# Second batch's dense layers in two chunks of 384 rows instead of three of 256

## The chip, the cores and the metric

The kernel runs on one core of one Trainium2 chip. The metric is the device time in microseconds; the time before is the median of three runs.

## The reference, cut to what matters

Three layers follow each other for a batch of 2, 768 rows each: an attention in which a row sees a window of earlier rows and the first few (sinks), a dense pair with a convolution over three neighbouring rows as a gate, and four attention experts of which each row uses two. The middle layer is the one that the change touches:

```
h = np.maximum(x @ w_in, 0.0)                    # x: 2 x 768 x 512, h: 2 x 768 x 1024
hp = pad h by one row of zeros on either side
for k in range(3):
    conv_out += conv_w[k][None, None, :] * hp[:, k:k + S, :]
gate = 1.0 / (1.0 + np.exp(-conv_out))
y = (h * gate @ w_out).astype(np.float32)        # 2 x 768 x 512
```

Then the third layer takes y: for each expert q, k, v by y @ wq[e], y @ wk[e], y @ wv[e], a causal softmax, @ v @ wo[e], weighted by a softmax over the two largest of four gate logits of the row.

## The kernel before

Features lie on the 128 partitions and rows run along the free axis. Every product of two matrices is made from three matmuls: both operands are split into a high part and a low part (`xh`, `xl`; `winhf`, `winlf`), and high x high, high x low and low x high are summed in one accumulator bank. The helper `hilo` makes such a pair: ScalarE copies the source into the high part, VectorE subtracts that from the source into the low part; `hilo_later` puts the subtraction on a list that is run one step later.

A batch's 768 rows are cut into chunks of CH = 256 rows. One **dense step** is one chunk c and one block f of 128 of the 1024 hidden features. Its parts are:

- H (`m1_H`, line 753): 4 input blocks x 3 = 12 matmuls of XW = 258 columns (256 rows and one neighbour on either side) into one bank. Then ScalarE does the relu (line 756) and, in the second batch, the product with the middle tap (line 758); in the first batch GpSimd has that product (line 760).
- conv (`m1_conv`): two VectorE instructions add the left and the right tap (lines 766, 767), then ScalarE's tanh (line 769).
- gate (`m1_gate`): VectorE forms (1 + tanh) x h (line 774), ScalarE copies it into the high part of g (line 776).
- rest (`m1_rest`, line 782): GpSimd makes the low part of g.
- Y (`m1_Y`, line 797): 4 output blocks of 128 x 3 = 12 matmuls of 256 columns into two banks, two output blocks in each, summed over the eight steps of the chunk. After the last one the sum is split into `yh` and `yl` (`hilo_later`, lines 130 and 131).

The order is written by hand: `run_phases` walks through steps and calls, at each step, the parts of all phases in the order of a list (ORD1), each part for its own step minus its lag. For the dense phase LAGM = (1, 2, 3) puts conv one step, gate two and rest three after the H of the same block, and LAG_Y puts its Y four after. So a step of this phase has one H, one conv, one gate and one Y of four different blocks. The first batch has 24 dense steps (its chunks in two halves of four blocks, so that weights can arrive late); the halves' sums are added on VectorE (line 815), cast on ScalarE (line 823), and the low part is taken on GpSimd (line 819). The second batch has 3 chunks x 8 blocks = 24 steps.

Beside the dense work `misc` runs at each step. From w0 = 32 on (i counts dense steps) it loads and splits the projections' weights, and at i = w0 it calls `narrow`: VectorE compares a guard tile and sums it (lines 188, 189), TensorE adds that over the partitions by one small matmul with a column of ones (line 191), and VectorE forms a flag from it (line 192). The flag decides at the end whether a second, general program has to run; it does not run here.

Buffers come from rings: W (18), R (15, for `xh`, `xl`, `yh`, `yl`), K (2 large ones, first the keys and later the projection weights), and eight accumulator banks (`psB`).

Of the kernel before, what the change touches and what calls it, by code (L numbers as in the profile page):

```python
# [29 lines left out]
E = 4  # L30
# [34 lines left out]
LAG_Y = 4  # L65
# [23 lines left out]
class Kernel:  # L89
# [508 lines left out]
    def xt(self, b, c):  # L598

        if (b, c) not in self.x:  # L600
            self.x[(b, c)] = (self.Rt([P, NKC, XW], s="xh"), self.Rt([P, NKC, XW], s="xl"))
            for edge, col in ((0, 0), (NCH - 1, XW - 1)):
                if c == edge:
                    for x in self.x[(b, c)]:
                        self.nc.gpsimd.memset(x[:, :, col : col + 1].bitcast(F32), 0.0)
        return self.x[(b, c)]

    def x_cols(self, qt):
        return slice(1 + (qt % 2) * P, 1 + (qt % 2 + 1) * P)

    def x_hi(self, b, qt, general=False):
        self.copy("a" if general else ENG_XH[b], self.xt(b, qt // 2)[0][:, :, self.x_cols(qt)], self.a1O[(b, qt)])

    def x_lo(self, b, qt, general=False):
        xh, xl = (x[:, :, self.x_cols(qt)] for x in self.xt(b, qt // 2))
        eng = self.nc.vector if general or ENG_X[b] == "d" else self.nc.gpsimd
        eng.tensor_tensor(xl, self.a1O.pop((b, qt)), xh.bitcast(F32), op=ALU.subtract)

    def x_halo(self, b, qt):
        c = qt // 2  # L620
        if qt % 2 == 0 and c > 0:
            for d, x in zip(self.xt(b, c - 1), self.xt(b, c)):
                self.nc.gpsimd.tensor_copy(d[:, :, XW - 1 : XW], x[:, :, 1:2])
        if qt % 2 == 1 and c < NCH - 1:
            for d, x in zip(self.xt(b, c + 1), self.xt(b, c)):
                self.nc.gpsimd.tensor_copy(d[:, :, 0:1], x[:, :, XW - 2 : XW - 1])

# [117 lines left out]
    def m1_H(self, b, c, f):  # L745
        nc = self.nc
        xh, xl = self.x[(b, c)]
# [6 lines left out]
        ht = self.Wt([P, XW + CH], s="ht")  # L754
        h, t1 = ht[:, :XW], ht[:, XW:]
        nc.scalar.activation(h, ps[:, :XW], AF.Relu, scale=0.5)  # L756
        if TAP == "a" or (TAP == "b" and b == 1):
            nc.scalar.mul(t1, h[:, 1 : 1 + CH], self.cw[:, NF + f : NF + f + 1])
        else:
            nc.gpsimd.tensor_scalar(t1, h[:, 1 : 1 + CH], self.cw[:, NF + f : NF + f + 1], 1.0, op0=ALU.mult, op1=ALU.mult)  # L760
        self.m1h[(b, c, f)] = (h, t1)

    def m1_conv(self, b, c, f):
        nc = self.nc
        h, t1 = self.m1h[(b, c, f)]
        nc.vector.scalar_tensor_tensor(t1, h[:, 0:CH], self.cw[:, f : f + 1], t1, op0=ALU.mult, op1=ALU.add)
        nc.vector.scalar_tensor_tensor(t1, h[:, 2 : 2 + CH], self.cw[:, 2 * NF + f : 2 * NF + f + 1], t1,  # L767
# [3 lines left out]
    def m1_gate(self, b, c, f):  # L771
        nc = self.nc
        h, t1 = self.m1h.pop((b, c, f))
        nc.vector.scalar_tensor_tensor(t1, t1, 1.0, h[:, 1 : 1 + CH], op0=ALU.add, op1=ALU.mult)  # L774
        g = self.Wt([P, 2, CH], F32R, "g")
        nc.scalar.copy(g[:, 0], t1)  # L776
        self.m1g[(b, c, f)] = (t1, g)

    def m1_rest(self, b, c, f):
        t1, g = self.m1g[(b, c, f)]  # L780
        eng = self.nc.vector if ENG_G[b] == "d" else self.nc.gpsimd
        eng.tensor_tensor(g[:, 1], t1, g[:, 0].bitcast(F32), op=ALU.subtract)  # L782
        self.m1g[(b, c, f)] = g

    def m1_Y(self, b, c, f):
# [6 lines left out]
        first, last = f == 0 or (halves and f == NF // 2), f == NF - 1 or (halves and f == NF // 2 - 1)  # L792
        if first:
            self.m1y = [self.psB().rearrange("p (a c) -> p a c", a=2) for _ in range(2)]
        for d in range(NKC):
            for i, (w, k) in enumerate(((wh, 0), (wh, 1), (wl, 0))):
                nc.tensor.matmul(self.m1y[d // 2][:, d % 2, :], w[:, f, d, :], g[:, k],  # L797
                                 start=(first and i == 0 and d % 2 == 0), stop=(last and i == 2),
                                 skip_group_check=True)
        if not last:  # L800
            return
# [26 lines left out]
    def mlp_phase(self, start):  # L828
# [29 lines left out]
        def each(fn):  # L858
# [430 lines left out]
```

## Time and profile before

| | before |
|---|---|
| median of 3 runs | 371.82 us (371.38 to 372.03) |
| profiled run | 371.99 us |
| its span | 370.1 us |
| TensorE busy | 359.7 us, 3166 matmuls |
| VectorE busy | 273.1 us |
| ScalarE busy | 261.2 us |
| GpSimd busy | 118.8 us |

The span is the time from the first to the last instruction on record; 1.9 us of the profiled run lie outside it. Matmuls overlap each other, so the time that one of them takes from the path is the distance from its start to the next one's start, not the duration in its row.

### The profile page before, as it was taken

How to read it: one execution, taken by the hardware profiler on the slowest of the kernel's cores; microseconds unless marked ns; L12 is line 12 of the kernel's file. 1: busy time of each engine (PE TensorE's matmuls, PEld its weight loads, DVE VectorE, ACT ScalarE, POOL GpSimd, SP SyncE). 2: the span in 40 equal slices, each digit the busy share in tenths (PEclk: the TensorE clock that was granted, in tenths of full speed). 3: DMA queues.
4: the chain of work that ended last, by engine and by line, in shares of the span. 5: the costliest groups of instructions: out<-in, count | busy, mean ns of one | idle time of the engine just before them, and what ended most of it. 6: DMA issues, size and time to landing. Idle time of an engine off the chain costs nothing.

```text
span 370.1 us, 8877 instructions
## 1 busy us (share of the span) xinstructions
PE 359.7 (97%) x3166; PEld 331.7 (90%) x3166; DVE 273.1 (74%) x850; ACT 261.2 (71%) x746; POOL 118.8 (32%) x230
## 2 busy tenths in 40 slices
PE   8999999899999999999999999999999999999994
PEld 5687877899899999999999999999999899978983
DVE  5689899999887997878756766238668688578731
ACT  4999998766886766546746766249878687849841
POOL 7014120444432342844421322500034144406310
PEclk9999999999999999999999999999999999999998
DMA  7943865353342311000211010000000010101112
GB/s 178 362 140 126 241 220 173 116 186 129 103 128 69 105 30 31 6 25 25 63 44 45 1 58 3 0 2 0 2 3 1 17 42 22 40 0 58 58 51 75
DMA packets 20404, 27.53 MB, mean 74 GB/s; under 512 B 2080, under 2 KB 12928, under 8 KB 20352
## 3 DMA queue, kind: packets, MB, share of 16 engines
q1 hardware_dynamic: 19120, 26.22, 22.2%
q10 hardware_dynamic: 1232, 0.66, 0.9%
q8 instruction: 27, 0.44, 0.5%
q14 instruction: 25, 0.20, 0.2%
HBM read 23.68 MB, written 3.19 MB: 73 GB/s over the span
## 4 chain that ended last, share of the span: by engine, by line
PE 77%; DVE 12%; ACT 5%; issue 2%; POOL 2%; DMA 1%; SPq 0%; ACTq 0%; DVEq 0%
PE psB L797 15%; PE psB L753 14%; PE psB L947 9%; PE psB L1061 5%; PE psB L1037 5%; PE psB L875 5%; PE psB L1085 4%; PE psB L587 4%; PE psB L484 4%; PE psB L545 3%; DVE P L486 3%; PE psB L1008 3%; PE psB L1007 3%; PE psB L471 2%; ACT P L489 2%
## 5 line engine op out<-in xcount | busy, mean ns | idle before, releaser
L797 PE MATMUL psB<-g,wouthf 128*128 128x256 f32 x384 | 70.5, 281 | 0.2 <-POOL g L782 0.2
L797 PEld LDWEIGHTS psB<-g,wouthf 128*128 128x128 f32 x384 | 58.9, 188 | 0.6 <-POOL g L782 0.4
L753 PE MATMUL psB<-xh,winhf 128*128 128x258 f32 x192 | 56.5, 294 | 0.0
L1025 POOL TENSOR_SCALAR P<-P,r 128x256 f32<-128x256 f32 (+5 forms) x48 | 30.3, 644 | 79.4 <-DVE r L1023 32.6
L753 PE MATMUL psB<-xh,winlf 128*128 128x258 f32 x192 | 54.3, 283 | 0.0
L753 PE MATMUL psB<-xl,winhf 128*128 128x258 f32 x192 | 54.2, 282 | 0.0
L797 PE MATMUL psB<-g,woutlf 128*128 128x256 f32 x192 | 53.8, 280 | 0.0
L489 ACT ACTIVATE P<-P,nm 128x260 f32<-128x260 f32 (+2 forms) x96 | 46.5, 486 | 10.1 <-DVE nm L486 9.9
L782 POOL TENSOR_TENSOR g<-ht,g 128x256 fp32r<-128x256 f32 x48 | 33.2, 691 | 52.4 <-ACT g L776 46.9
L1014 ACT ACTIVATE P<-P,nm 128x256 f32<-128x256 f32 (+5 forms) x48 | 32.1, 669 | 13.5 <-DVE nm L1013 7.8
L769 ACT ACTIVATE ht<-ht 128x256 f32<-128x256 f32 x48 | 20.1, 418 | 28.3 <-DVE ht L767 28.2
L774 DVE SCALAR_TENSOR_TENSOR ht<-ht 128x256 f32<-128x256 f32 x48 | 24.2, 505 | 18.8 <-ACT ht L769 18.8
L753 PEld LDWEIGHTS psB<-xh,winhf 128*128 128x128 f32 x192 | 36.4, 189 | 0.3 <-ACT ht L756 0.2
L753 PEld LDWEIGHTS psB<-xl,winhf 128*128 128x128 f32 x192 | 36.5, 190 | 0.0
L753 PEld LDWEIGHTS psB<-xh,winlf 128*128 128x128 f32 x192 | 36.2, 189 | 0.0
L797 PEld LDWEIGHTS psB<-g,woutlf 128*128 128x128 f32 x192 | 36.2, 189 | 0.0
L1010 DVE CUSTOM_DVE_ANT_0 P<-psB,causal 128x384 f32<-128x384 f32 (+3 forms) x64 | 30.3, 503 | 5.7 <-PE psB L1008 5.2
L760 POOL TENSOR_SCALAR ht<-ht,cw 128x256 f32<-128x256 f32 x24 | 15.1, 627 | 59.8 <-ACT ht L756 52.3
L767 DVE SCALAR_TENSOR_TENSOR ht<-ht,cw 128x256 f32<-128x256 f32 x48 | 28.3, 589 | 1.7
L545 PE MATMUL psB<-ident,P 128*128 128x128 f32 x176 | 29.0, 281 | 0.2
L947 PE MATMUL psB<-yh,wqh 128*128 128x256 f32 x96 | 27.2, 283 | 0.0
L947 PE MATMUL psB<-yl,wqh 128*128 128x256 f32 x96 | 27.0, 281 | 0.0
(172 smaller groups left out, 961.3 us busy)
## 6 DMA issues: line engine op xcount, KB each, us to landing
raw<-in_w_in_dram SPq DMA_DIRECT2D x8, 512.0 KB, 4.1
raw<-in_w_out_dram SPq DMA_DIRECT2D x8, 512.0 KB, 3.3
v<-in_v_dram SPq DMA_DIRECT2D x12, 256.0 KB, 4.4
R<-rD SPq DMA_DIRECT2D x24, 128.0 KB, 2.9
out_dram<-ot SPq DMA_DIRECT2D x11, 256.0 KB, 2.0
k<-in_k_dram SPq DMA_DIRECT2D x7, 260.0 KB, 3.6
raw<-in_wqkv_dram SPq DMA_DIRECT2D x8, 193.0 KB, 3.0
q<-in_q_dram SPq DMA_DIRECT2D x6, 256.0 KB, 4.5
```

The costliest lines, as they stand in the source:

```text
L489: nc.scalar.activation(Pt[:, j, :N], Pt[:, j, :N], AF.Exp, bias=nmx[:, j : j + 1], scale=-1.0, accum_out=sums[:, j : j + 1])
L545: nc.tensor.transpose(ps[:, j, c, :], Pt[:, j, c0 : c0 + P], self.ident)
L753: nc.tensor.matmul(ps[:, :XW], w[:, f, kc, :], x[:, kc, :], start=(i == 0), stop=(i == len(ops) - 1))
L767: nc.vector.scalar_tensor_tensor(t1, h[:, 2 : 2 + CH], self.cw[:, 2 * NF + f : 2 * NF + f + 1], t1, op0=ALU.mult, op1=ALU.add)
L769: nc.scalar.activation(t1, t1, AF.Tanh)
L774: nc.vector.scalar_tensor_tensor(t1, t1, 1.0, h[:, 1 : 1 + CH], op0=ALU.add, op1=ALU.mult)
L782: eng.tensor_tensor(g[:, 1], t1, g[:, 0].bitcast(F32), op=ALU.subtract)
L797: nc.tensor.matmul(self.m1y[d // 2][:, d % 2, :], w[:, f, d, :], g[:, k], start=(first and i == 0 and d % 2 == 0), stop=(last and i == 2), ...
L947: nc.tensor.matmul(ps, w[:, kc, c0 : c0 + P], y[:, kc, :], start=(i == 0), stop=(i == len(ops) - 1))
L1010: nc.vector.tensor_tensor_reduce(out=Pt[:, lo:hi], in0=ps[:, : hi - lo], in1=mask, scale=-1.0, scalar=BIG, op0=ALU.add, op1=ALU.min, accum ...
L1014: nc.scalar.activation(Pt[:, :N], Pt[:, :N], AF.Exp, bias=nm[:, 0:1], scale=-1.0, accum_out=sums[:, j : j + 1])
L1025: nc.gpsimd.tensor_scalar(Ps[j][:, :N], Ps[j][:, :N], r[:, j : j + 1], 1.0, op0=ALU.mult, op1=ALU.mult)
```

## The change

In the second batch a chunk has 384 rows (`TPC` = 3 tiles of 128 instead of 2), so there are 2 x 8 = 16 dense steps instead of 24. H has 386 columns, Y has 384 and one bank for each output block, four banks instead of two. Each bank is drained in two pieces, 256 and 128 columns, since `yh` and `yl` stay cut by 256 rows, and the subtraction is made at once instead of a step later. The second batch's lags are (0, 1, 2, 3): the convolution of a block comes in the step of its own H. `w0` is four steps earlier, 28 instead of 32, and with it `narrow`. The phase is cut into m (first batch), n (second batch) and z (`misc` and background work).

The rest is about room: the second chunk's x lies in one large K buffer that held keys, its first chunk's x in tiles of two input blocks each, `h`, `t` and the two parts of g in buffers of their own, the low projection weights in three R tiles, the first batch's queries in the K buffer after x, all values in one pool, the zeros in W. The neighbour columns of x are copied when the tile on the right is there, both directions at once.

```diff
-LAGM = (1, 2, 3)
+LAGM = ((1, 2, 3, 4), (0, 1, 2, 3))
     def x_halo(self, b, qt):
...
+        c, n = qt // TPC[b], TPC[b] * P
+        if qt % TPC[b] or c == 0:
+            return
+        for ls, rs in zip(self.xt(b, c - 1), self.xt(b, c)):
+            for (g, l), (_, r) in zip(ls, rs if len(rs) == len(ls) else [(0, rs[0][1][:, g : g + l.shape[1]]) for g, l in ls]):
+                self.nc.gpsimd.tensor_copy(l[:, :, n + 1 : n + 2], r[:, :, 1:2])
+                self.nc.gpsimd.tensor_copy(r[:, :, 0:1], l[:, :, n : n + 1])
     def m1_H(self, b, c, f):
...
+        n = TPC[b] * P
-            nc.tensor.matmul(ps[:, :XW], w[:, f, kc, :], x[:, kc, :], start=(i == 0), stop=(i == len(ops) - 1))
+            nc.tensor.matmul(ps[:, : n + 2], w[:, f, kc, :], x[kc], start=(i == 0), stop=(i == len(ops) - 1))
     def m1_Y(self, b, c, f):
...
+        per = 1 if b else 2
         if first:
-            self.m1y = [self.psB().rearrange("p (a c) -> p a c", a=2) for _ in range(2)]
+            self.m1y = [self.psB()[:, : per * TPC[b] * P].rearrange("p (a c) -> p a c", a=per) for _ in range(NKC // per)]
...
+        if b:
+            tiles = range(c * TPC[b], (c + 1) * TPC[b])
...
+            for d in range(NKC):
+                for k in sorted({t // 2 for t in tiles}):
+                    mine = [t for t in tiles if t // 2 == k]
+                    dst = slice(mine[0] % 2 * P, (mine[-1] % 2 + 1) * P)
+                    src = self.m1y[d][:, 0, (mine[0] - tiles[0]) * P : (mine[-1] + 1 - tiles[0]) * P]
+                    yh, yl = self.y[(b, k)]
+                    self.hilo(src, yh[:, d, dst], yl[:, d, dst])
+            return
     def mlp_phase(self, start):
...
-        steps += [(1, c, f) for c in range(NCH) for f in range(NF)]
-        w0 = NSTEP + NF
+        steps1 = [(1, c, f) for c in range(NT // TPC[1]) for f in range(NF)]
+        w0 = NSTEP + NF // 2
...
-            if w0 + 3 <= i < w0 + 3 + 2 * NKC:
-                self.hilo_later(*self.wraw.pop(i - w0 - 3))
+            if w0 + 2 <= i < w0 + 2 + 2 * NKC:
+                for part in self.wraw.pop(i - w0 - 2):
+                    self.hilo_later(*part)
...
+        n0 = start + len(steps)
+        total = len(steps) + len(steps1)
+        z = {"more": (0, more), "misc": (0, misc)}
+        return (phase(start, steps, LAGM[0]), phase(n0, steps1, LAGM[1]),
+                lambda names: (start, total, [z[n] for n in names.split()], 1), start + total)
```

What stands in a row on VectorE around the guard, before. L766 and L767 are the two convolution instructions, L774 the gate, L188 and L189 the guard, L192 the flag; the block whose tile is `ht_2845` had its H one step earlier than the H that TensorE has just done:

```order
L774 SCALAR_TENSOR_TENSOR ht_2810<-ht_2810 128x256 [waits Activation_49]
L766 SCALAR_TENSOR_TENSOR ht_2845<-ht_2845,cw 128x256 [waits Pool_49]
L767 SCALAR_TENSOR_TENSOR ht_2845<-ht_2845,cw 128x256 [waits DVE_49]
L188 TENSOR_SCALAR guard<-guard 128x17
L189 TENSOR_REDUCE g_2901<-guard 128x1 [waits DVE_49]
L192 SCALAR_TENSOR_TENSOR flag<-psB_2904,c_831 1x1 [waits PE_49]
```

And in the changed kernel, where L785 and L786 are the convolution, L794 the gate, L189, L190 and L193 the guard and the flag; `t_2774` belongs to the H that TensorE has just done, and L852 adds the halves of the first batch's last chunk:

```order
L852 TENSOR_TENSOR y_2078<-psB_2593,y_2078 128x512 [waits PE_49]
L852 TENSOR_TENSOR y_2078<-psB_2594,y_2078 128x512 [waits PE_49]
L785 SCALAR_TENSOR_TENSOR t_2715<-h_2714,cw,t_2715 128x384 [waits Activation_49]
L786 SCALAR_TENSOR_TENSOR t_2715<-h_2714,cw,t_2715 128x384 [waits DVE_49]
L794 SCALAR_TENSOR_TENSOR t_2715<-t_2715,h_2714 128x384 [waits Activation_49]
L785 SCALAR_TENSOR_TENSOR t_2774<-h_2773,cw,t_2774 128x384 [waits Activation_49]
L786 SCALAR_TENSOR_TENSOR t_2774<-h_2773,cw,t_2774 128x384 [waits DVE_49]
L189 TENSOR_SCALAR guard<-guard 128x17
L190 TENSOR_REDUCE g_2798<-guard 128x1 [waits DVE_49]
L193 SCALAR_TENSOR_TENSOR flag<-psB_2801,c_831 1x1 [waits PE_49]
```

The guard stands behind two convolutions in both; what moved is whose convolutions they are, those of the H of the step before, or of this step's own.

On TensorE at the same place, before, the end of a Y (L797), the small matmul (L191) and the next H (L753):

```order
L797 MATMUL psB_2743<-g_2814,wouthf 128x256 x2
L797 MATMUL psB_2743<-g_2814,woutlf 128x256
L797 MATMUL psB_2743<-g_2814,wouthf 128x256 x2
L797 MATMUL psB_2743<-g_2814,woutlf 128x256
L191 MATMUL psB_2904<-ones,g_2901 1x1 [waits DVE_49,PE_49]
L753 MATMUL psB_2912<-xh_1592,winhf 128x258
```

And in the changed kernel, a Y (L822), the small matmul (L192) and the next H (L768):

```order
L822 MATMUL psB_2740<-g_2681,woutlf 128x384
L822 MATMUL psB_2741<-g_2681,wouthf 128x384
L822 MATMUL psB_2741<-g_2682,wouthf 128x384
L822 MATMUL psB_2741<-g_2681,woutlf 128x384
L192 MATMUL psB_2801<-ones,g_2798 1x1 [waits DVE_49,Activation_49]
L768 MATMUL psB_2811<-xh_1244,winhf 128x386 [waits PE_49]
```

The small matmul keeps its place between a Y and the next H; the Y ahead of it has 384 columns in each matmul instead of 256.

## Rows read from the trace of the kernel before

**Rows 1.** Page, parts 1 and 2: busy us (share) xinstructions; granted clock in tenths.

```profile
PE 359.7 (97%) x3166; PEld 331.7 (90%) x3166; DVE 273.1 (74%) x850; ACT 261.2 (71%) x746; POOL 118.8 (32%) x230
...
PEclk9999999999999999999999999999999999999998
```

**Rows 2.** Page, part 4: chain that ended last, by engine.

```profile
PE 77%; DVE 12%; ACT 5%; issue 2%; POOL 2%; DMA 1%; SPq 0%; ACTq 0%; DVEq 0%
```

**Rows 3.** Windows: stretch, length, then busy us (instructions) by engine, clock, DMA.

```profile
183.00:230.00 47.00, 47.00 (x397) 46.84 (x396) 30.84 (x66) 30.42 (x78) 11.04 (x16) 1.00 0.12 34
```

**Rows 4.** Timeline, TensorE, an H group: start us, duration us, instruction.

```profile
227.56 0.28 PE L753 MATMUL psB<-xh,winhf 128*128 128x258 f32 x1
...
229.00 0.40 PE L797 MATMUL psB<-g,wouthf 128*128 128x256 f32 x2
```

**Rows 5.** Timeline, TensorE, third layer: 256, 384 and 512 columns.

```profile
293.60 0.28 PE L947 MATMUL psB<-yh,wqh 128*128 128x256 f32 x1
...
295.02 0.82 PE L1037 MATMUL psB<-ident,P 128*128 128x128 f32 x6
...
295.86 0.34 PE L1008 MATMUL psB<-KS,QL 128*128 128x384 f32 x1
...
297.10 0.28 PE L947 MATMUL psB<-yh,wqh 128*128 128x256 f32 x1
...
299.87 0.63 PE L1085 MATMUL psB<-wohf,zh 128*128 128x512 f32 x2
...
301.27 0.34 PE L1007 MATMUL psB<-KS,QH 128*128 128x384 f32 x1
...
301.97 0.28 PE L947 MATMUL psB<-yh,wqh 128*128 128x256 f32 x1
```

**Rows 6.** Timeline, VectorE, around the guard.

```profile
185.97 0.48 DVE L767 SCALAR_TENSOR_TENSOR ht<-ht,cw 128x256 f32<-128x256 f32 x1
...
186.57 0.17 DVE L189 TENSOR_REDUCE g<-guard 128x1 f32<-128x17 f32 x1
```

**Rows 7.** Timeline, TensorE, around the small matmul.

```profile
183.05 0.40 PE L797 MATMUL psB<-g,wouthf 128*128 128x256 f32 x2
...
187.21 0.28 PE L797 MATMUL psB<-g,woutlf 128*128 128x256 f32 x1
187.41 0.19 PE L191 MATMUL psB<-ones,g 128*1 128x1 f32 x2
```

**Rows 8.** Timeline, ScalarE, at a convolution, an H and a chunk end.

```profile
164.97 0.42 ACT L769 ACTIVATE ht<-ht 128x256 f32<-128x256 f32 x1 [2.44 <-DVE ht L767]
...
183.31 0.39 ACT L756 ACTIVATE ht<-psB 128x258 f32<-128x258 f32 x1 [0.45 <-PE psB L753]
...
218.96 1.07 ACT L130 CAST yh<-psB 128x512 fp32r<-128x512 f32 x2
221.81 0.42 ACT L769 ACTIVATE ht<-ht 128x256 f32<-128x256 f32 x1 [1.78 <-DVE ht L767]
```

**Rows 9.** Groups, ScalarE, 183 to 230 us: xcount | busy us, mean ns.

```profile
L758 ACT ACTIVATE ht<-ht,cw 128x256 f32<-128x256 f32 x17 | 8.7, 512 | 0.6
...
L130 ACT CAST wqh<-raw 128x386 fp32r<-128x386 f32 x8 | 4.0, 499 | 0.0
```

**Rows 10.** Groups, VectorE, the same stretch.

```profile
L131 DVE TENSOR_TENSOR wql<-raw,wqh 128x386 fp32r<-128x386 f32 x8 | 4.5, 558 | 0.0
L131 DVE TENSOR_TENSOR yl<-psB,yh 128x512 fp32r<-128x512 f32 x4 | 2.6, 686 | 4.4 <-ACT yh L130 4.4
```

**Rows 11.** Timeline, VectorE, beside the low parts on GpSimd.

```profile
162.24 1.25 DVE L766 SCALAR_TENSOR_TENSOR ht<-ht,cw 128x256 f32<-128x256 f32 x1
163.53 1.41 DVE L767 SCALAR_TENSOR_TENSOR ht<-ht,cw 128x256 f32<-128x256 f32 x1
```

**Rows 12.** Timeline, GpSimd, the low parts of one chunk.

```profile
161.90 2.75 POOL L819 TENSOR_TENSOR yl<-y,yh 128x512 fp32r<-128x512 f32 x2 [0.48 <-ACT yh L823]
```

**Rows 13.** Timeline, GpSimd, a copy of neighbour columns.

```profile
137.22 0.38 POOL L626 CAST xl<-xl 128x4 fp32r<-128x4 f32 x1 [0.76 <-DVE xl L617]
```

More of the change, by code (lines that the diff above doesn't have):

```diff
@@ L64 @@
 RATE1 = 1.1
-LAG_Y = 4
 NP2BUF = 8
@@ L600, in xt @@
         if (b, c) not in self.x:
-            self.x[(b, c)] = (self.Rt([P, NKC, XW], s="xh"), self.Rt([P, NKC, XW], s="xl"))
-            for edge, col in ((0, 0), (NCH - 1, XW - 1)):
+            w = TPC[b] * P + 2
+            if b and c:
+                t = self.Kt([P, 2, NKC, w], F32R, "x")
+                self.x[(b, c)] = [[(0, t[:, i])] for i in range(2)]
+            else:
+                n = NKC if b == 0 else NKC // 2
+                self.x[(b, c)] = [[(g, self.Rt([P, n, w], s="x" + s)) for g in range(0, NKC, n)] for s in "hl"]
@@ L619, in x_halo @@
+        self.a1O.pop((b, qt))
     def x_halo(self, b, qt):
[L620 to L626, printed above, removed]
+        c, n = qt // TPC[b], TPC[b] * P
+        if qt % TPC[b] or c == 0:
+            return
@@ L746, in m1_H @@
         nc = self.nc
-        xh, xl = self.x[(b, c)]
+        xh, xl = ([x[:, i] for _, x in part for i in range(x.shape[1])] for part in self.x[(b, c)])
         wh, wl = self.win
@@ L773, in m1_gate @@
         h, t1 = self.m1h.pop((b, c, f))
-        nc.vector.scalar_tensor_tensor(t1, t1, 1.0, h[:, 1 : 1 + CH], op0=ALU.add, op1=ALU.mult)
-        g = self.Wt([P, 2, CH], F32R, "g")
-        nc.scalar.copy(g[:, 0], t1)
+        n = TPC[b] * P
+        nc.vector.scalar_tensor_tensor(t1, t1, 1.0, h[:, 1 : 1 + n], op0=ALU.add, op1=ALU.mult)
+        if b:
+            g = [self.Wt([P, n], F32R, "g") for _ in range(2)]
+        else:
+            g = self.Wt([P, 2, n], F32R, "g")
+            g = [g[:, i] for i in range(2)]
+        nc.scalar.copy(g[0], t1)
         self.m1g[(b, c, f)] = (t1, g)
@@ L856, in more, with phase, each @@
             self.background(BG2 // 2)
-        def each(fn):
-            return lambda i: fn(*steps[i])
-        st = {"more": (0, more), "rest": (LAGM[2], each(self.m1_rest)), "gate": (LAGM[1], each(self.m1_gate)), "conv": (LAGM[0], each(self.m1_conv)),
-              "H": (0, each(self.m1_H)), "Y": (LAG_Y, each(self.m1_Y)), "misc": (0, misc)}
-        return lambda names: (start, len(steps), [st[n] for n in names.split()], 1)
+        def phase(start, steps, lags):
+            def each(fn):
+                return lambda i: fn(*steps[i])
+            conv, gate, rest, Y = lags
+            st = {"rest": (rest, each(self.m1_rest)), "gate": (gate, each(self.m1_gate)), "conv": (conv, each(self.m1_conv)),
+                  "H": (0, each(self.m1_H)), "Y": (Y, each(self.m1_Y))}
+            return lambda names: (start, len(steps), [st[n] for n in names.split()], 1)
+        n0 = start + len(steps)
[3 more added lines that the diff above has]
+                lambda names: (start, total, [z[n] for n in names.split()], 1), start + total)
     def vg_unit(self, b, tt):
@@ L871, in vg_unit @@
         ts_ = slice(tt % 2 * P, (tt % 2 + 1) * P)
-        c0 = 2 * E * D
         ops = [(y, w, kc) for kc in range(NKC) for y, w in ((yh, wh), (yh, wl), (yl, wh))]
         for i, (y, w, kc) in enumerate(ops):
-            nc.tensor.matmul(ps[:, :NVG], y[:, kc, ts_], w[:, kc, c0 : c0 + NVG], start=(i == 0),
+            nc.tensor.matmul(ps[:, :NVG], y[:, kc, ts_], w[2][:, kc], start=(i == 0),
                              stop=(i == len(ops) - 1))
@@ L943, in qk_unit @@
         ps = self.psB()[:, :CH]
-        c0 = which * E * D + p * P
+        cols = slice(p * P, (p + 1) * P)
         ops = [(w, y, kc) for kc in range(NKC) for w, y in ((wh, yh), (wh, yl), (wl, yh))]
         for i, (w, y, kc) in enumerate(ops):
-            nc.tensor.matmul(ps, w[:, kc, c0 : c0 + P], y[:, kc, :], start=(i == 0), stop=(i == len(ops) - 1))
+            nc.tensor.matmul(ps, w[which][:, kc, cols], y[:, kc, :], start=(i == 0), stop=(i == len(ops) - 1))
         cs = slice(c * CH, (c + 1) * CH)
@@ L1211, in program @@
             if general:
-                ph = [m("rest gate conv H"), late, m("Y misc more")]
+                ph = [m("rest gate"), n("rest"), m("conv H"), n("H gate conv"), late, m("Y"), n("Y"), z("misc more")]
             else:
                 a0, a1 = first
-                src = {"a0": a0, "a1": a1, "m": m, "late": late}
+                src = {"a0": a0, "a1": a1, "m": m, "n": n, "z": z, "late": late}
                 ph = self.order(ORD1, src)
```

83 lines of the change are left out of this document (49 added, 34 removed).

## The prediction

> **What bounds the kernel now.** I read the busy table first, then the chain that ended last, then the windows of the changed stage, and only then single rows. TensorE is busy 359.7 of 370.1 us and its clock row is full nearly everywhere [rows 1]; 77% of the chain is TensorE [rows 2]. In the window from 183 to 230 us, which lies inside the second batch's dense steps, TensorE is busy 47.00 of 47.00 us with 397 matmuls at a granted clock of 1.00, while VectorE has 30.84, ScalarE 30.42 and GpSimd 11.04 us of work [rows 3]. So in this stage time can be won only where a matmul starts earlier after the one before it, and lost only where TensorE is made to wait. What the other engines are spared is worth nothing by itself.
>
> A matmul's own duration (0.28 us) overlaps its neighbours', so I price matmuls by the distance of starts. An H group of twelve 258-column matmuls takes from 227.56 to 229.00 us, 1.44 us: 120.0 ns each [rows 4]. Twelve 256-column matmuls of the query projection take from 293.60 to 295.02 us: 118.3 ns [rows 5]. For 384 columns the same view has four from 301.27 to 301.97 us, 175 ns each, and seven from 295.86 to 297.10 us, 177 ns; for 512 columns six from 299.87 to 301.27 us, 233.3 ns [rows 5]. From 256 to 512 columns that is 115.0 ns for 256 columns, 0.449 ns a column, which leaves 3.4 ns that do not depend on the columns. By that line 384 columns take 175.8 ns, between the two rows, and 386 take 176.7.
>
> **Part 1, fewer and wider matmuls.** H had 3 chunks x 8 blocks x 12 = 288 matmuls at 120.0 ns, 34.56 us; it has 192 at 176.7 ns, 33.93 us: 0.63 us less. Y had 288 at 118.3 ns, 34.07 us; it has 192 at 175.8 ns, 33.75 us: 0.32 us less. Together 0.95 us. With 175 ns for 384 columns (175.9 for 386) it is 0.79 + 0.47 = 1.26 us; with 177 ns (177.9) 0.40 + 0.09 = 0.49 us. I take 0.95 and keep 0.5 to 1.3 us. All of it lies on the path, since TensorE is full there.
>
> **Part 2, the check on the guard.** The sum over the guard that decides whether the kernel's narrow path was valid ends in one small matmul. The feeding step (counted in dense steps) moves from i = 32 to i = 28, and at the same time the convolution of a block comes in the step of its own H (lag 0, it was 1). Before, the two convolution instructions and the two guard instructions on VectorE belonged to an H that was a whole step old: the reduce ran at 186.57 us for 0.17 us, to 186.74 [rows 6], and TensorE came to the small matmul at 187.41 us [rows 7], 0.67 us later. That matmul cost little more than a gap of 0.2 us.
>
> After, the same reduce stands behind both convolutions of the block whose H has just been computed. The chain from the start of the Y group that follows this H: ScalarE's relu starts 0.26 us after Y's first matmul (183.31 against 183.05) [rows 7, 8]. Relu on 386 columns: a 386-column ScalarE cast takes 499 ns [rows 9], so 0.50. Tap product: 512 ns at 256 columns [rows 9]; from 258 to 386 columns ScalarE's price rises by 0.11 us, from the relu of 0.39 at 183.31 us to that cast [rows 8, 9], so 0.62. Two convolutions: 0.48 us at 256 columns [rows 6]; VectorE's step from 386 to 512 columns is 558 to 686 ns, 0.13 [rows 10], so 0.61 each. Then the guard, 0.29 from the convolution's end at 186.45 to 186.74 [rows 6]. With 0.03 to 0.04 for each of four handovers (tanh at 164.97 us after a convolution that ended at 164.94 is one [rows 8, 11]) the sum is 0.26 + 0.50 + 0.62 + 0.61 + 0.61 + 0.29 + 0.14 = 3.03 us, and some 0.07 more until TensorE starts. TensorE has 12 Y matmuls x 175.8 ns = 2.11 us to do in that time, then it stands at the small matmul, and the next H is queued behind it: **a wait of 1.0 us even if ScalarE and VectorE are in step**.
>
> They may not be. Just before this step GpSimd computes the low parts of the first batch's last chunk; beside the same work on the chunk before (161.90 us, two instructions, 2.75 us) two convolutions took 1.25 and 1.41 us instead of 0.48 [rows 6, 11, 12]. Followed by hand with the new step lengths, that work ends about when the guard's convolutions begin, so a part of a stretched convolution is left over: 1.4 us. If both convolutions were stretched by 0.7 the wait would be 2.4 us. I take 1.2, between the floor and the hand-made chain, and keep 1.0 to 2.4 us. It could be below 1.0 only if TensorE were later than I count or VectorE's order other than the one shown above; a gain I exclude, since the 0.2 us gap of before is what is left to win there.
>
> The Trainium skill, in GPSIMD Engine Reference, "8. Key points", states that GpSimd shares its SBUF interfaces with VectorE and contends with VectorE instructions that have two SBUF inputs. The stretched convolutions (two SBUF inputs, 0.48 to 1.41 us) agree with it, and it would put the wait at the upper end, 2.4 us, if the overlap were full.
>
> **Part 3, edits that I cost at nothing.** Chunk boundary: two casts of 512 columns (1.07 us together [rows 8]) and two subtractions (0.69 us each [rows 10]) become eight and eight pieces on four banks; ScalarE and VectorE take turns on a bank, about 1.1 us a bank by the same rows scaled to 256 and 128 columns, 4.0 us in all. Before, the next tanh came at 221.81 us, 2.85 us after the casts began at 218.96 [rows 8]. After, the next gate values are ready about 9.2 us after the last Y, and their Y stands two and a half steps of 4.23 us on, at 10.6: 1.4 us of cover. If the drain were longer than that, TensorE would wait for the excess. Halo copies, now eight small pieces in one go, cost 8 x 0.38 = 3.0 us of GpSimd at most by the slower of their rows [rows 13], which is busy for a third of the span [rows 1]. At the end of the stage TensorE passes on to the first batch's projections, which read nothing of these chunks. The extra cast and subtraction for x in halves, the loads in 512 and 260 columns, the values in their own buffers and the queries in the key buffer are off TensorE; its rows there keep their order, and their waits are for work long done. The loads on SP come four steps earlier, in front of nothing that TensorE lacks.
>
> **Sum.** 0.95 saved, 1.2 lost: +0.25 us. The profiled run took 371.99 us (370.1 span and 1.9 outside it), so 372.24 on its scale; the median of the runs is 371.82, so **372.1 us**. The case's own range: -1.26 + 1.0 = -0.3 to -0.49 + 1.4 = +0.9, 371.5 to 372.7.
>
> **The rivals.**
> - *The wait is hidden.* VectorE's chain is shorter than I add up, or TensorE has other matmuls between Y and the check. Then the 0.95 stand alone: **370.9 us**. For it: before, the same check was free by 0.67 us. Against it: the order rows, where nothing stands between. It needs the wait to be under 0.2 us to be seen as faster.
> - *GpSimd stretches both convolutions* (slower): wait 2.4 us, **373.3 us**. It decides from 1.7 us of wait on (0.95 + 0.74). For it: the stretched rows [rows 11]; against it: by the chain most of GpSimd's work ends before.
> - *The drain of four banks outlasts its 1.4 us of cover*: its price is the excess; the nearest row is the 2.85 us that the old drain held the next tanh back, and if the new one held it back by twice that, 5.7 instead of 4.0, the excess would be 5.7 - 4.0 - 1.4 = 0.3 us, once: 372.4 us.
> - *The price of a matmul hardly depends on its columns.* Then 192 fewer matmuls are won whole: 192 x 118.3 ns = 22.7 us, **349.1 us**. Against it: 118, 176 and 233 ns for 256, 384 and 512 columns [rows 5]. The Trainium skill, in TensorE: Matmul & The Clock Gate, "Back-to-back issue gap", gives about 81 ns for 128 and 131 ns for 512 columns in a stream of weight loads and matmuls; an estimate on that page's line (98 and 114 ns for 256 and 384) saves 12.7 us, 359.1 us. The rows differ from the page (233 against 131 ns at 512 columns), and the measurement decides.
>
> **How the numbers follow.** About 0.2% (0.74 us) is what a measurement of this kernel can tell from no change: faster is below 371.1, slower above 372.6. Forecast 0.55, of which 0.05 lies above 372.6; hidden wait 0.20; stretched convolutions 0.17, of which 0.03 stays below 372.6 where the stretch is partial; drain 0.05; cheap matmuls 0.03. Faster: 0.20 + 0.03 = 0.23. Slower: 0.05 + 0.14 + 0.03 (drains that add up with a long check) = 0.22. The rest, 0.55, is the same. The range leaves out the cheap matmuls and the outer halves of the two sides: 370.8 to 373.3.
>
> **What would show it.** In the profile after: H and Y at 176 to 177 ns from start to start in the second batch; one idle stretch of TensorE of 1.0 to 1.4 us at about 182 us, released by the guard's reduce on VectorE; no wait of TensorE at the chunk boundary; span longer by about 0.25 us. A wait at the check under 0.3 us, or spacing outside 171 to 179 ns, would make the prediction wrong, and so would a second wait.

## The result and the profile after

The changed kernel takes 375.89 us (median of 6 runs, 374.65 to 377.44) beside 371.81 us before (6 runs, 371.38 to 372.28): ratio 1.0115, 95% interval 1.0088 to 1.0141. It is slower by 4.1 us; 372.1 was predicted, and the range ended at 373.3. The profiled run took 375.66 us with a span of 373.7.

The busy table and the clock row of the page, which answer to [rows 1]:

```profile
PE 360.1 (96%) x2974; PEld 331.8 (89%) x2974; DVE 276.4 (74%) x843; ACT 257.8 (69%) x731; POOL 118.8 (32%) x224
...
PEclk9999999999999999999989999999999999999999
```

There are 192 matmuls fewer, and in the slice from 187 to 196 us the clock row has an 8 that the row before did not have. The chain that ended last has less TensorE in it, 67% where [rows 2] had 77%, and more VectorE, 19% for 12%:

```profile
PE 67%; DVE 19%; ACT 6%; issue 3%; POOL 2%; DMA 1%; ACTq 0%; DVEq 0%; POOLq 0%
```

TensorE's list of waits (us in total, times, longest) has one new first line:

```profile
PE psB L192 <- DVE g L190: 2.9, 1, 2.9
```

The place in TensorE's timeline, answering to [rows 7] (start us, duration us, in brackets the idle time and what ended it):

```profile
182.38 0.34 PE L822 MATMUL psB<-g,woutlf 128*128 128x384 f32 x1
185.66 0.19 PE L192 MATMUL psB<-ones,g 128*1 128x1 f32 x2 [2.94 <-DVE g L190]
185.78 0.69 PE L768 MATMUL psB<-xh,winhf 128*128 128x386 f32 x1
...
188.84 0.35 PE L768 MATMUL psB<-xh,winhf 128*128 128x386 f32 x1
...
189.38 0.51 PE L822 MATMUL psB<-g,wouthf 128*128 128x384 f32 x2
...
191.48 0.34 PE L768 MATMUL psB<-xh,winhf 128*128 128x386 f32 x1
...
193.61 0.51 PE L822 MATMUL psB<-g,wouthf 128*128 128x384 f32 x2
```

TensorE stands idle for 2.94 us at the small matmul. Idle time counts from the modelled end of the matmul before; from start to start the small matmul is 3.10 us late (185.66 - 182.38, less the usual 0.18). The H behind it then takes 185.78 to 189.38, 3.60 us, where the next one takes 191.48 to 193.61, 2.13 us (177 ns a matmul). The windows over the same stretch (start and end, length, then busy us by engine, clock, DMA) show the clock:

```profile
182.56:185.66 3.10, 0.16 (x1) 0.03 (x1) 2.78 (x5) 1.53 (x3) 1.15 (x2) 0.96 0.29 85
185.78:188.84 3.06, 3.06 (x11) 3.06 (x10) 0.61 (x2) 0.00 (x0) 0.00 (x0) 0.50 0.00 0
188.84:193.61 4.77, 4.77 (x28) 4.77 (x28) 2.17 (x3) 2.04 (x4) 1.02 (x1) 1.00 0.03 8
```

After the idle stretch the granted clock is 0.50 of full speed (1.2 GHz) up to 188.84 us, then 1.00 again. That costs 3.60 - 2.13 = 1.47 us on top of the wait.

**The account.** I measure the stage from the first H of the second batch to the first query projection. Before: 160.99 to 244.75 us, 83.76 us. After: 161.61 to 248.88, 87.27 us, 3.51 more. The rows of these four starts, two before and two after:

```profile
160.99 0.28 PE L753 MATMUL psB<-xh,winhf 128*128 128x258 f32 x1
...
244.75 0.28 PE L947 MATMUL psB<-yh,wqh 128*128 128x256 f32 x1
```

```profile
161.61 0.34 PE L768 MATMUL psB<-xh,winhf 128*128 128x386 f32 x1
...
248.88 0.28 PE L991 MATMUL psB<-yh,wqh 128*128 128x256 f32 x1
```

And the stage begins 0.62 us later, 0.55 of it lost between 93.7 and 105.8 us, in a part of the program where TensorE's order is the same. Together that is 4.13 us; from there to the last matmul both kernels take the same time to 0.02 us. (The span differs by only 3.6 us because the tail from the start of the last matmul on, 5.3 us before and 4.8 after, was shorter.)

### The profile page after: what moved, and what is told of

Read it like the earlier page. It is cut to its first block, busy times and chain, and to the rows that moved or that the text cites. A ratio compares the mean times of both kernels' runs of the same rounds, so it can differ in the third digit from the quotient of the medians.

```text
span 373.7 us, 8472 instructions
## 1 busy us (share of the span) xinstructions
PE 360.1 (96%) x2974; PEld 331.8 (89%) x2974; DVE 276.4 (74%) x843; ACT 257.8 (69%) x731; POOL 118.8 (32%) x224
## 4 chain that ended last, share of the span: by engine, by line
PE 67%; DVE 19%; ACT 6%; issue 3%; POOL 2%; DMA 1%; ACTq 0%; DVEq 0%; POOLq 0%
PE psB L822 12%; PE psB L768 10%; PE psB L991 9%; PE psB L1107 5%; PE psB L1083 5%; PE psB L922 5%; PE psB L1131 4%; PE psB L588 4%; PE psB L485 3%; DVE P L487 3%; PE psB L546 3%; PE psB L1054 2%; PE psB L1053 2%; DVE ht L786 2%; DVE ht L785 2%
## 5 line engine op out<-in xcount | busy, mean ns | idle before, releaser
L822 PE MATMUL psB<-g,wouthf 128*128 128x256 f32 (+1 forms) x320 | 68.5, 304 | 0.2 <-POOL g L806 0.2
L822 PEld LDWEIGHTS psB<-g,wouthf 128*128 128x128 f32 x320 | 52.8, 188 | 0.9 <-POOL g L806 0.7
L822 PE MATMUL psB<-g,woutlf 128*128 128x256 f32 (+1 forms) x160 | 48.4, 303 | 0.0
L768 PE MATMUL psB<-xh,winhf 128*128 128x258 f32 (+1 forms) x128 | 40.8, 319 | 0.1
L768 PE MATMUL psB<-xh,winlf 128*128 128x258 f32 (+1 forms) x128 | 38.5, 301 | 0.0
L768 PE MATMUL psB<-xl,winhf 128*128 128x258 f32 (+1 forms) x128 | 38.5, 301 | 0.0
L806 POOL TENSOR_TENSOR g<-t,g 128x384 fp32r<-128x384 f32 x16 | 17.0, 1065 | 48.4 <-ACT g L800 36.3
L822 PEld LDWEIGHTS psB<-g,woutlf 128*128 128x128 f32 x160 | 30.1, 188 | 0.0
L991 PE MATMUL psB<-yh,wql 128*128 128x256 f32 x96 | 27.0, 281 | 0.0
L502 ACT COPY PT<-psB 128x512 f32<-128x512 f32 (+1 forms) x48 | 25.5, 531 | 0.8 <-PE psB L546 0.8
L768 PEld LDWEIGHTS psB<-xh,winhf 128*128 128x128 f32 x128 | 24.8, 194 | 0.6 <-ACT ht L774 0.4
L768 PEld LDWEIGHTS psB<-xl,winhf 128*128 128x128 f32 x128 | 24.7, 193 | 0.0
L768 PEld LDWEIGHTS psB<-xh,winlf 128*128 128x128 f32 x128 | 24.6, 192 | 0.0
```

What stands on the lines that cost most here:

```text
L502: self.nc.scalar.copy(dst, src)
L768: nc.tensor.matmul(ps[:, : n + 2], w[:, f, kc, :], x[kc], start=(i == 0), stop=(i == len(ops) - 1))
L822: nc.tensor.matmul(self.m1y[d // per][:, d % per, :], w[:, f, d, :], g[k], start=(first and i == 0 and d % per == 0), stop=(last and i == ...
L991: nc.tensor.matmul(ps, w[which][:, kc, cols], y[:, kc, :], start=(i == 0), stop=(i == len(ops) - 1))
```

## The experiments

### Take the wait away, move it, fill it, relieve it

`e1_split` leaves the guard's VectorE instructions where they are and issues the small matmul one dense step later:

```diff
             if i == w0 and self.halves:
                 self.narrow()
+            if i == w0 + 1 and self.halves:
+                self.narrow2()
     def narrow(self):
...
         nc.vector.tensor_reduce(g, ok, axis=AX.X, op=ALU.add)
+        self.gsum = g
+
+    def narrow2(self):
+
+        nc = self.nc
+        g = self.gsum
         ps = self.psB()[0:1, 0:1]
         nc.tensor.matmul(ps, g, self.ones, start=True, stop=True)
```

> The guard's two VectorE instructions stay in their place (dense step 28); the small matmul and the flag go one dense step later. Theory (TensorE stood at the small matmul for 2.9 us, and then ran at half its clock for a while): the reduce is long done, no wait, no fall of the clock, and what is left is the wider matmuls' saving: 4.4 us less than the changed kernel, 371.0 to 371.6 us. Rival (the loss comes mostly from elsewhere, the wait is only where it shows, since ScalarE and VectorE are behind and the next gate values would be late in its stead): the wait moves to a Y group, and the time stays above 373.5 us.

`e2_later` moves the whole check back to its old place:

```diff
-            if i == w0 and self.halves:
+            if i == w0 + 4 and self.halves:
                 self.narrow()
```

> The whole check at dense step 32 again, as in the kernel before; convolution still in the step of its own H. Theory (a floor of about 1.0 us from the order, the rest from GpSimd's low parts of the first batch's last chunk, which are over by then): wait 1.0 to 1.7 us there, the clock does not fall or falls for a shorter time, 372.5 to 373.3 us. Rival (the order alone makes the whole wait of 2.9 us): again 2.9 us, 375 to 376 us.

`e3_fill` puts dummy matmuls ahead of the small one (nothing reads them):

```diff
+        full = self.psB()
+        ps = full[0:1, 0:1]
+        for _ in range(16):
+            nc.tensor.matmul(full[:, :384], self.win[0][:, 0, 0, :], self.x[(1, 0)][0][0][1][:, 0, :384], start=True, stop=True)
         nc.tensor.matmul(ps, g, self.ones, start=True, stop=True)
```

> Sixteen 384-column matmuls whose result is thrown away stand ahead of the small matmul, 2.8 us of work for TensorE in the time in which it stood idle. Theory (the idle stretch makes the clock fall, and that costs about 1.4 us on top of the wait): the wait is nearly gone as idle time, its length is not, the clock stays at its full level, the twelve 386-column matmuls behind it take 177 ns each again, 1.4 us less than the changed kernel: 374.0 to 374.8 us. Rival (the slow twelve matmuls after the wait have another cause than idleness): same time as the changed kernel, 375.5 to 376.5 us.

`e4_lowlate` defers GpSimd's low parts of the first batch's last chunk by three steps:

```diff
-                self.later.append(lo)
+                f = lo
+                for _ in range(3 if c == NCH - 1 else 0):
+                    f = lambda f=f: self.later.append(f)
+                self.later.append(f)
```

> GpSimd's low parts of the first batch's last chunk come three dense steps later; the rest is the changed kernel. Theory (beside them the convolutions of the step before and ScalarE's relu behind them are about 1.3 us late): wait of 1.3 to 1.9 us instead of 2.9, the fall of the clock is in doubt: 372.8 to 374.6 us. Rival (the low parts only run beside a chain that is late anyway): wait unchanged within 0.3 us, 375.5 to 376.5 us.

Measured, with 371.94 us for the kernel before on the chip of the four variants (371.81 for the changed kernel):

| | median us | ratio (95%) | idle at the small matmul | stage us |
|---|---|---|---|---|
| changed kernel | 375.89 | 1.0115 (1.0088 to 1.0141) | 2.94 | 87.27 |
| e1_split | 371.88 | 1.0000 (0.9990 to 1.0010) | none | 82.90 |
| e2_later | 373.10 | 1.0034 (1.0022 to 1.0046) | 1.39 | 84.34 |
| e3_fill | 374.54 | 1.0068 (1.0048 to 1.0087) | none (filled) | 85.86 |
| e4_lowlate | 375.14 | 1.0088 (1.0057 to 1.0119) | 1.93 | 86.92 |

The small matmul in four more profiled runs, in the order e4_lowlate and e2_later, then e7_rest_dve and e8_both of the next section:

```profile
184.87 0.19 PE L192 MATMUL psB<-ones,g 128*1 128x1 f32 x2 [1.93 <-DVE g L190]
...
201.52 0.19 PE L192 MATMUL psB<-ones,g 128*1 128x1 f32 x2 [1.39 <-DVE g L190]
...
200.69 0.19 PE L192 MATMUL psB<-ones,g 128*1 128x1 f32 x2 [0.73 <-DVE g L190]
...
184.48 0.19 PE L192 MATMUL psB<-ones,g 128*1 128x1 f32 x2 [1.09 <-DVE g L190]
```

In e1_split's timelines of VectorE and then TensorE, with the first and the last row of its stage around, the reduce is done 1.3 us before TensorE comes to the small matmul, and a gap of 0.27 us from start to start is all that is left:

```profile
185.60 0.17 DVE L190 TENSOR_REDUCE g<-guard 128x1 f32<-128x17 f32 x1
```

```profile
161.84 0.34 PE L774 MATMUL psB<-xh,winhf 128*128 128x386 f32 x1
...
186.83 0.34 PE L828 MATMUL psB<-g,woutlf 128*128 128x384 f32 x1
187.10 0.19 PE L198 MATMUL psB<-ones,g 128*1 128x1 f32 x2
187.22 0.45 PE L774 MATMUL psB<-xh,winhf 128*128 128x386 f32 x1
...
244.74 0.28 PE L999 MATMUL psB<-yh,wqh 128*128 128x256 f32 x1
```

No Y waits in its place, so the rival of a loss from elsewhere falls: 87.27 - 82.90 = 4.37 us of the stage hang on the place of the small matmul and of the flag behind it alone. What is left of the stage is 83.76 - 82.90 = 0.86 us shorter than before: the wider matmuls' saving, nearly as predicted (0.95). It is net of a small second loss: where two Y groups follow each other at the end of the last chunk they take 4.42 us in the changed kernel and 4.44 in e1_split, waiting for a low part of g from GpSimd, and 4.20 in e7_rest_dve, where VectorE makes it. But the run is not 0.9 us faster than the kernel before, only level with it, 0.3 us above what I expected: the 0.55 us lost ahead of the stage are still there.

e3_fill ended as the theory said: the reduce still ends as late, and the small matmul starts at 185.63 us as in the changed kernel (185.66). The time in which TensorE stood is as long as before, but filled, and the clock does not fall (windows of e3_fill):

```profile
182.00:186.00 4.00, 3.88 (x24) 3.53 (x23) 3.37 (x7) 2.19 (x5) 1.78 (x2) 1.00 0.22 66
186.00:189.00 3.00, 3.00 (x18) 3.00 (x18) 0.47 (x2) 0.73 (x2) 0.00 (x0) 1.00 0.00 0
```

It is 1.35 us faster than the changed kernel (375.89 to 374.54; the stage in the traces 1.41), with more work: that is the price of the fallen clock. The one run of the changed kernel with a mean clock of 0.999, 374.65 us, lies where e3_fill does.

In e4_lowlate the idle time goes to 1.93 us, a full 1.0 less, so GpSimd's low parts do make a part of it. The stage is only 0.35 us shorter, and the median, 375.14, lies above what was expected. Two things ate the rest in the profiled run. The clock still fell: the first H matmuls behind the wait start 178 ns apart, from 186.15 us on 322 ns apart, and the H and the Y after it take 3.09 and 2.76 us, 1.6 more than at the full clock (1.47 in the changed kernel). And the two Y groups at the end of the last chunk take 4.94 us instead of 4.42, with an idle time of 0.50 us for a low part of g. Not every run lost its clock: the run with a mean clock of 1.000 took 373.90 us, those at 0.994 and 0.995 took 375.5 and 375.9, one at 0.989 took 377.56. The mean clock is a coarse sign: the kernel before, which has no such wait, has runs from 0.994 to 1.000 in no order with their times, and the changed kernel's five runs at 0.994 or 0.995 spread from 375.5 to 377.4 us.

### Which part of the wait comes from where

`e6_early` is the kernel before with the check alone at step 28; `e7_rest_dve` is e2_later with the second batch's low part of g on VectorE; `e8_both` is the changed kernel with e4_lowlate's and e7_rest_dve's edits and the check at step 28, where the changed kernel has it. Their edits, first that of e6_early, then the one that e7_rest_dve and e8_both add:

```diff
-            if i == w0 and self.halves:
+            if i == NSTEP + NF // 2 and self.halves:
                 self.narrow()
...
-ENG_G = 'pp'
+ENG_G = 'pd'
```

> The kernel before, with the check alone moved from dense step 32 to 28; the convolution still comes one step after its H, three chunks of 256 rows. With e2_later (order changed, place not) and the changed kernel (both) it makes a table of two by two. Theory (place and order each make a part of the wait: GpSimd's low parts stretch VectorE's queue there): wait 0.8 to 1.3 us, no fall of the clock, 372.6 to 373.3 us. Rival (the place is harmless while the convolution is a step old): wait under 0.3 us, 371.7 to 372.2 us.

> The kernel of e2_later with the second batch's low part of g on VectorE instead of GpSimd. In e2_later the second convolution before the check took 1.23 us beside GpSimd's 1.03 us product, the first 0.62 us alone. Theory (GpSimd beside it stretches it, and the floor of the wait is the chain without that): the convolution takes 0.62 us, the wait at the check falls from 1.4 to 0.7 to 0.9 us, 372.3 to 372.8 us. Rival (the second convolution is slow for a reason of its own, such as the columns that it reads): it stays at 1.2 us and the wait at 1.3 us or more, 373.0 to 373.6 us.

> The changed kernel with the check in its place (dense step 28), GpSimd's low parts of the first batch's last chunk three steps later, as in e4_lowlate, and the second batch's low part of g on VectorE, as in e7_rest_dve. Theory (the idle 2.9 us are a sum: 0.7 in step, as in e7_rest_dve; 0.7 from GpSimd beside the second convolution, e2_later less e7_rest_dve; 1.0 from the low parts, the changed kernel less e4_lowlate; 0.5 from other work on VectorE there): idle 1.1 to 1.5 us, the clock stays up in most runs, 372.7 to 373.4 us. Rival (the parts do not add: VectorE with one more instruction a step stays behind): idle 1.8 us or more, 373.9 us or more.

Measured: e6_early 377.74 us (372.19 before on that chip), ratio 1.0144 (1.0128 to 1.0161), idle 3.58 us; e7_rest_dve 372.28 us, 1.0003 (0.9993 to 1.0014), idle 0.73; e8_both 372.91 us (372.16 before), 1.0023 (1.0007 to 1.0038), idle 1.09.

e7_rest_dve isolates the product on GpSimd. VectorE's two convolutions and the reduce before the small matmul, first in e2_later:

```profile
199.29 0.62 DVE L785 SCALAR_TENSOR_TENSOR t<-h,cw,t 128x384 f32<-128x384 f32 x1 [0.75 <-ACT t L776]
199.94 1.23 DVE L786 SCALAR_TENSOR_TENSOR t<-h,cw,t 128x384 f32<-128x384 f32 x1
...
201.30 0.17 DVE L190 TENSOR_REDUCE g<-guard 128x1 f32<-128x17 f32 x1
```

then what GpSimd did meanwhile there:

```profile
199.74 1.03 POOL L806 TENSOR_TENSOR g<-t,g 128x384 fp32r<-128x384 f32 x1 [3.11 <-ACT g L800]
```

and VectorE in e7_rest_dve:

```profile
199.07 0.62 DVE L785 SCALAR_TENSOR_TENSOR t<-h,cw,t 128x384 f32<-128x384 f32 x1 [1.50 <-ACT t L776]
199.72 0.62 DVE L786 SCALAR_TENSOR_TENSOR t<-h,cw,t 128x384 f32<-128x384 f32 x1
...
200.46 0.17 DVE L190 TENSOR_REDUCE g<-guard 128x1 f32<-128x17 f32 x1
```

The same convolution takes 1.23 us beside GpSimd's product and 0.62 alone, and the idle time falls from 1.39 to 0.73. With e4_lowlate the idle 2.94 us of the changed kernel come apart like this: 0.73 with all engines in step; 0.66 from GpSimd's product beside the second convolution (1.39 - 0.73); 1.01 from its low parts (2.94 - 1.93); and 0.54 from other work that keeps VectorE behind at step 28 (1.93 - 1.39; the sum of the first batch's halves, 1.28 us, stands in its row there, but no run takes it away by itself). e8_both tests the sum: 0.73 + 0.54 = 1.27 expected, 1.09 measured. So the parts add, to 0.2 us.

e6_early is the miss of the study: 3.58 us of idle where 0.8 to 1.3 were expected, and the clock at half for longer. Its TensorE and VectorE rows, and the window after:

```profile
175.68 0.28 PE L797 MATMUL psB<-g,woutlf 128*128 128x256 f32 x1
179.54 0.19 PE L191 MATMUL psB<-ones,g 128*1 128x1 f32 x2 [3.58 <-DVE g L189]
```

```profile
175.03 1.40 DVE L767 SCALAR_TENSOR_TENSOR ht<-ht,cw 128x256 f32<-128x256 f32 x1
176.91 0.92 DVE L774 SCALAR_TENSOR_TENSOR ht<-ht 128x256 f32<-128x256 f32 x1 [0.48 <-ACT ht L769]
177.76 0.47 DVE L766 SCALAR_TENSOR_TENSOR ht<-ht,cw 128x256 f32<-128x256 f32 x1
178.27 0.49 DVE L767 SCALAR_TENSOR_TENSOR ht<-ht,cw 128x256 f32<-128x256 f32 x1
```

```profile
179.66:184.97 5.31, 5.31 (x27) 5.31 (x26) 2.11 (x6) 1.51 (x4) 0.64 (x1) 0.50 0.00 0
```

In VectorE's row each step's convolution stands behind the gate of the block before, the gate behind ScalarE's tanh, and that behind the convolution of the block before. So one stretched convolution (1.40 us beside the low parts, which run from 174.68 us for 2.87) moves everything behind it. Counting H groups and convolution pairs from the start of the second batch, the pair at 177.76 belongs to the H that TensorE began at 170.05 us, 7.7 us earlier. A convolution that is "a step old" was therefore no cover at this place. The two by two table, idle us at the small matmul:

| | check at step 32 | check at step 28 |
|---|---|---|
| 3 chunks, convolution one step after its H | no wait (a gap of 0.2; the kernel before) | 3.58 (e6_early) |
| 2 chunks, convolution in the step of its H | 1.39 (e2_later) | 2.94 (changed kernel) |

**The place alone makes a wait of 3.6 us, the new order with its wider chunks one of 1.4.** (No run separates the order from the width.) They don't add. In e6_early the convolution ahead of the check starts 7.7 us after its H, where 3.9 is usual later in that kernel; in the changed kernel it starts 4.9 us after its H (178.32 to 183.24), where 3.5 is usual. So VectorE lags less there. That the longer dense step makes this (4.23 us with 384 rows, 2.86 with 256) is likely, but no run tests it.

### The 0.55 us ahead of the stage

`e5_copies` is e1_split with two copies that nothing reads, where the kernel before copied neighbour columns. `e9_split` and `e10_copies` are e1_split and e5_copies again, side by side on one chip.

```diff
         c, n = qt // TPC[b], TPC[b] * P
+        if b and qt == 1:
+            for x in self.xt(b, c):
+                pad = self.pSm.tile([P, 2, 1], F32, tag="pad", name=self.nm("pad"))
+                self.nc.gpsimd.tensor_copy(pad, x[0][1][:, :, 2 * P : 2 * P + 1].bitcast(F32))
         if qt % TPC[b] or c == 0:
             return
```

> The kernel of e1_split with two small GpSimd copies into a scratch tile put where the kernel before copied the neighbour columns of the second batch's first chunk (97.6 us in its trace); nothing reads them. In all five traces of the changed kernel and its variants TensorE loses about 0.55 us against the kernel before between 96 and 106 us. Theory (without those copies GpSimd's product for g starts beside a convolution on VectorE, which takes 0.90 instead of 0.48 us, and everything behind it is late): the loss in that stretch shrinks from 0.55 to 0.1 to 0.2 us, and the time goes to 371.3 to 371.6 us. Rival (the extra cast and subtraction for x in halves make the loss): it stays at 0.5 us or more, 371.8 to 372.3 us.

> The kernel of e1_split again, beside e10_copies on one chip. Theory: the wider matmuls' 0.86 us gained less 0.55 us lost ahead of them, 0.2 to 0.4 us under the kernel before. Rival: no difference from the kernel before, ratio 1.000.

> The kernel of e5_copies again, beside e9_split on one chip. Theory (the two small copies on GpSimd give back 0.35 to 0.4 us ahead of the dense stage): 0.3 to 0.5 us under e9_split, 0.5 to 0.9 us under the kernel before. Rival (e5_copies was 0.8 us under it by the chip's scatter): within 0.2 us of e9_split.

Measured: e5_copies 371.37 us (12 runs; before 372.19 on that chip), 0.9980 (0.9969 to 0.9991); e9_split 371.86 us and e10_copies 370.99 us (before 372.16), 0.9991 (0.9982 to 1.0000) and 0.9965 (0.9951 to 0.9978).

VectorE and then GpSimd near 98 us in e1_split:

```profile
98.10 0.90 DVE L792 SCALAR_TENSOR_TENSOR ht<-ht,cw 128x256 f32<-128x256 f32 x1
```

```profile
98.09 0.63 POOL L812 TENSOR_TENSOR g<-ht,g 128x256 fp32r<-128x256 f32 x1
```

and in e5_copies:

```profile
98.26 0.48 DVE L796 SCALAR_TENSOR_TENSOR ht<-ht,cw 128x256 f32<-128x256 f32 x1
```

```profile
98.22 0.18 POOL L644 COPY pad<-xh 128x2 f32<-128x2 f32 x1
98.34 0.45 POOL L644 COPY pad<-xl 128x2 f32<-128x2 f32 x1
98.75 0.83 POOL L816 TENSOR_TENSOR g<-ht,g 128x256 fp32r<-128x256 f32 x1
```

In e1_split GpSimd's product starts with the convolution and stretches it from 0.48 to 0.90 us. With the two copies ahead of it on GpSimd it starts when the convolution is over. ScalarE's tanh waits for that convolution, and behind the tanh stands the copy that makes the next operand of TensorE's first-layer matmuls: it starts at 99.02 us in the kernel before and at 99.69 in the changed one. From the first layer's group of 24 matmuls at 94.08 us to the H at 105.83, e5_copies takes 11.75 us; the kernel before took 93.63 to 105.21, 11.58; the changed kernel 93.72 to 105.84, 12.12. The ends of the stretch, before and after:

```profile
93.63 1.53 PE L587 MATMUL psB<-PT,v 128*64 128x128 f32 x24
...
105.21 0.39 PE L753 MATMUL psB<-xh,winhf 128*128 128x258 f32 x1
```

```profile
93.72 1.53 PE L588 MATMUL psB<-PT,v 128*64 128x128 f32 x24
...
105.84 0.39 PE L768 MATMUL psB<-xh,winhf 128*128 128x258 f32 x1
```

So 0.37 of 0.54 us come back, and the rest, 0.17, may go with x in halves, whose casts take 0.70 us for 0.61 and subtractions 0.76 for 0.69 in the same stretch; a wait of TensorE for ScalarE at 95.8 us is 0.69 instead of 0.61 there. That part I have not tested by itself. e9_split lies 0.30 us under the kernel before, as 0.86 gained and 0.55 lost would have it; e1_split, the same kernel, was level with it, so a difference of this size is at the edge of what the runs can tell. Side by side e10_copies is 0.87 us under e9_split, where 0.3 to 0.5 were expected: more than the 0.55 by which its trace is ahead at the end of the stage (244.14 against 244.69 us) and more than the 0.37 that the copies explain; the rest may be scatter (5 runs). e10_copies beats the kernel before by 1.17 us and is the best version found.

## Why the prediction was wrong, point by point

- **What bounds the kernel, and part 1**: right. H at 177 ns from start to start, Y at 176 (193.61 us on), forecast 176.7 and 175.8; the saving in the stage is 0.86 us, forecast 0.95, between the ends 0.5 and 1.3.
- **Part 2, the mechanism**: right as far as it goes. The wait is at the small matmul, released by the guard's reduce, where the prediction put it, and its floor "in step" holds: in e7_rest_dve the small matmul starts 3.00 us after Y's first matmul (197.69 to 200.69 us), forecast 3.03 and 0.07; less the 2.11 us of Y that is a delay of 0.89, forecast 1.0. What it left out is the place, as the next point says.
- **Part 2, the size**: this is the first step that failed. I took 1.2 and kept up to 2.4; it was 2.94 idle, 3.10 from start to start. Two terms were short. The product on GpSimd (0.66) was left out: I used 0.48 us convolutions from rows where GpSimd was silent, though the change puts convolution and product in step. And the low parts with VectorE's lag got 0.4 us (the 1.4 of the hand-made chain less the 1.0 of the floor), where the runs show 1.01 + 0.54. The sentence behind it, that the low parts end "about when the guard's convolutions begin", came out true (182.72 and 183.24 us); the error was to take VectorE as in step again from there on. The pair before, stretched to 1.24 and 1.54 us, had already made everything behind it late. The trace of before held the warning: there too the pair for the H of 170.08 us starts at 177.75, more than two steps of 2.86 us behind, and I read the lag only at step 32 [rows 6, 7]. Hence the argument that the order makes the wait was incomplete too: the place would have made one without it.
- **The fallen clock** was in no part and no rival, the second step that failed: 1.35 us by e3_fill, 1.47 by the H behind the wait. I priced a wait at its own length.
- **Part 3, edits costed at nothing**: right for the chunk boundary. The drain ran from 212.22 us for 4.5 us (forecast 4.0) and no Y waited there (a Y at the end of the stage lost 0.2). Wrong for the halo copies and x in halves: 0.55 us. I asked what the eight copies in one go would cost on GpSimd, and not what happens where two copies are taken away: the product behind them comes earlier and runs into a convolution.
- **The rivals**: stretched convolutions came nearest, with its place and sign, but not as written: of the guard's own pair only the second was stretched (0.62 and 1.32 us), and by the product for g, not by the low parts, which had stretched the second of the pair before (1.54 us; 0.62 in e4_lowlate). At 373.3 us it was still 2.6 short of the median, by the clock (1.4), the early loss (0.55) and the rest of the wait (0.6). It had a chance of 0.17. The hidden wait and the long drain did not come. Cheap matmuls fell: the widths cost what [rows 5] said.

ScalarE's drain in the profile of the changed kernel, its first piece, the last one and the tanh that it holds back:

```profile
212.22 0.36 ACT L124 CAST yh<-psB 128x256 fp32r<-128x256 f32 x1
...
216.16 0.27 ACT L124 CAST yh<-psB 128x128 fp32r<-128x128 f32 x1 [0.49 <-DVE yl L127]
218.30 0.52 ACT L788 ACTIVATE t<-t 128x384 f32<-128x384 f32 x1 [1.88 <-DVE t L786]
```

The account in one line: -0.86 (wider matmuls) + 4.37 (the check: 2.94 idle, about 1.4 at half clock) + 0.55 (ahead of the stage) = 4.06 us, where the medians differ by 4.08.

## What to carry to other kernels

Where a saturated TensorE meets one small matmul that waits for a long VectorE chain, split the two: leave the chain where it is and issue the matmul a step later (4.0 us here, from 375.89 to 371.88). Before moving such a check, read at the new place, not the old one, how far the engines behind TensorE lag. And when an edit takes small instructions off an engine in a tight schedule, look at what then starts earlier, and beside what.

## What the runs showed of the hardware

- A wait of TensorE can cost more than its length. After 2.94 us idle the granted clock was at 0.50 (1.2 GHz) for the next 3.1 us of the row and an H took 3.60 us instead of 2.13; after 3.58 us idle it was at 0.50 for 5.3 us; after 1.93 us idle it fell in the profiled run, 1.2 us after TensorE had resumed, and not in every run (one had a mean of 1.000); in the profiled runs with 1.39, 1.09 and 0.73 us idle it stayed at 1.00 behind the wait, though one run each of e2_later and e8_both shows a mean of 0.993 and a time 1.4 and 1.6 us above the median. The same stretch filled with matmuls whose result nobody reads kept it at 1.00.
- A VectorE instruction with two SBUF inputs is slowed by an elementwise product that GpSimd runs beside it: a convolution of 384 columns took 0.62 us alone and 1.23 beside a 1.03 us product on GpSimd. The Trainium skill (GPSIMD Engine Reference, "8. Key points") states this contention; these rows agree and put a factor of two on it.
- Work that nobody needs made a kernel faster: two copies of 0.18 and 0.45 us on GpSimd gave back 0.37 us of TensorE's time by holding a later instruction off VectorE's.
